# Windowed attention ahead of two expert layers: the transposes move into the scores' banks

## The chip, the cores and the metric

One core of one Trainium2 chip. The metric is the device time of one execution in microseconds (us), the median over the runs shown. Engines: PE is TensorE (PEld its weight loads), DVE is VectorE, ACT is ScalarE, POOL is GpSimd, SP is the engine that issues most DMAs.

## The reference, cut to what matters

```python
def _attn_ref(q, k, v):                       # (2, 8, 576, 64) each
    scores = (1 / np.sqrt(D)) * np.matmul(q, k.transpose(0, 1, 3, 2))
    # heads 0-3: 0 <= i - j < 32; heads 4-7: 0 <= i - j < 128 and (i - j) % 4 == 0
    scores = np.where(masks[None], scores, -1000000000.0)
    scores = scores - np.max(scores, axis=-1, keepdims=True)
    attn = np.exp(scores)
    attn = attn / (np.sum(attn, axis=-1, keepdims=True) + 1e-09)
    return np.matmul(attn, v)
def _moe_ref(x, domain_probs, w1, w2):        # x: 1152 x 512, 4 experts of 1024
    p = domain_probs / (domain_probs.sum(-1, keepdims=True) + 1e-09)
    return sum(p[:, e:e + 1] * (np.maximum(x @ w1[e], 0) @ w2[e]) for e in range(4))
def _moe2_ref(x, w_in, w_out, a, b):          # 512 -> 2048 -> 512
    h = x @ w_in
    P = a[0] + a[1] * h + a[2] * h**2 + a[3] * h**3
    Q = 1 + abs(b[0]) * abs(h) + abs(b[1]) * h**2
    return (P / (Q + 1e-06)) @ w_out
# output = _moe2_ref(_moe_ref(attention, 1152 x 512))
```

## The kernel before, in words

The 1152 tokens are cut into three chunks c of 384, the 8 heads into four pairs p. Attention works on twelve units (c, p), one chunk and two heads each (j = 0, 1). Since every query sees only a short band of keys, a unit is cut into 6 blocks of 64 queries by 96 keys (pairs 0 and 1) or 8 blocks of 48 queries by 80 keys (pairs 2 and 3, whose keys are gathered with step 4). Two blocks lie above each other on the 128 partitions, so a unit's scores are 128 x 2 x 288 or 128 x 2 x 320 values.

A unit goes through these steps, methods of `Attn`: `load` and `load_values` (SP issues the DMAs of queries with keys, L199, and of values, L206); `scores` on PE (L217) into the two PSUM banks `ps_s`, one a head; `masked` on DVE (L230), which adds a mask that is 0 or a large negative number and writes `pr` in SBUF; `maxima` on DVE (L240, and L241, which multiplies by minus the scale); `exps` on ACT (L248), one instruction a block pair and head, with the sums of the rows; `norm` (reciprocals on DVE, L255 and L256, two multiplications on POOL, L258); `transposes` of one head on PE (L269) into a bank of the pool `pso`; `copies` of that head back to SBUF, head 0 on DVE, head 1 on ACT (L275); `values` on PE (L286) into another `pso` bank; `split`, a rounded copy xh on ACT (L304, L311) and the rest xl = ps_v - xh on DVE (L306, L312).

PSUM has eight banks: two for `ps_s`, two for `pso` (tag "o", shared by transposes, value products and the output tiles `ps_o` of L363), four for the hidden layer `ps_h` (L326).

The order on every engine is that of the code, written by hand: an engine runs its instructions in the order in which the program issues them and waits in place. The units are pipelined over rounds r = 0 to 13 (L585): in round r unit r has its exponentials, unit r + 1 its scores, mask and maxima, unit r - 1 its transposes, unit r - 2 its value product and split. `keep_warm(n)` (L553) issues n dummy matmuls whose result nobody reads. Into the rounds are woven, by two tables, the first blocks of the next layer: `fill` (PE blocks of 12 matmuls, the hidden layer `h_k` and `hb`, L326, from round 3 on, and output tiles `o_tile`, L363, from round 8 on) and `prep` (splitting weights into a rounded part, L104, on DVE for the first two weight units and on ACT later, and a rest, L105, on DVE; and the loads of later weights). `late` is a list of deferred steps, among them the relu pair of L339 (hh, ACT) and L340 (hl, DVE); `run_late` issues what it holds.

After the last round the two expert layers run with the same blocks, PE nearly without a pause.

Of the kernel before, what the change touches and what calls it, by code (L numbers as in the profile page):

```python
# [18 lines left out]
F32 = mybir.dt.float32  # L19
# [15 lines left out]
TC = 384  # L35
# [9 lines left out]
def body(ctx, tc, qkv, mask, dp, w1, w2, w1d, w2d, coef, out):  # L45
# [45 lines left out]
    def split_w(store, nm):  # L91
        raws = {}

        def split(u, halves=(0, 1)):
            if u >= 2 * NG1:
                return
            if halves[0] == 0:
                raws[u] = store[u]
                store[u] = wp.tile([128, 2, 1024], F32R, tag=nm, name=nm)
            raw, w = raws[u], store[u]  # L100
            for i in halves:
                s = slice(i * 512, (i + 1) * 512)

                (nc.vector.tensor_copy if nm == "w1" and u < 2 else nc.scalar.copy)(w[:, 0, s], raw[:, s])  # L104
                nc.vector.tensor_tensor(  # L105
                    out=w[:, 1, s], in0=raw[:, s], in1=w[:, 0, s].bitcast(F32), op=ALU.subtract
                )
        return split
# [72 lines left out]
    class Attn:  # L181
# [5 lines left out]

        def __init__(self, c, p):
            self.c, self.p = c, p
            self.half = {}  # L190
            self.nb, self.qb, self.kb = BLOCKS[p // 2]
            self.n = self.nb // 2 * self.kb

# [31 lines left out]
            return t.rearrange("p (j i) -> p j i", j=2)  # L225

        def masked(self):
            pr = self.pr = ap.tile([128, 2, 320], F32, tag="pr", name="pr")[:, :, :self.n]
            m = mask_sb[:, 2 * (self.p // 2) + (self.c == 1), :self.n]
            nc.vector.tensor_tensor(  # L230
                out=pr, in0=ps_s[:, :, :self.n],
                in1=m.rearrange("p (o n) -> p o n", o=1).to_broadcast([128, 2, self.n]), op=ALU.add,
            )

        def blocks(self):
            return self.pr.rearrange("p j (i k) -> p j i k", k=self.kb)

        def maxima(self):
            mx, self.nmx = self.small("mx"), self.small("nmx")
            nc.vector.reduce_max(mx, self.blocks(), axis=AX.X)  # L240
            nc.vector.tensor_scalar_mul(self.nmx, mx, -QSCALE)  # L241

        def exps(self):
            self.total = self.small("total")
            pr = self.blocks()
            for j in range(2):
                for i in range(self.nb // 2):
                    nc.scalar.activation(  # L248
                        pr[:, j, i], pr[:, j, i], AF.Exp, scale=QSCALE, bias=self.nmx[:, j, i:i + 1],
                        accum_out=self.total[:, j, i:i + 1],  # L250
                    )

# [10 lines left out]

        def transposes(self, j):
            pr = self.blocks()
            ps = pso.tile([128, 512], F32, tag="o", name="ps_t")[:self.kb, :64 * self.nb]
            for i in range(self.nb // 2):
                n = 64 + self.qb
                nc.tensor.transpose(ps[:, i * 128:i * 128 + n], pr[:n, j, i], ident[:n, :n])  # L269
            self.half[j] = ps  # L270

        def copies(self, j):
            pt = ap.tile([96, TC], F32, tag=f"pt{j}", name="pt", bufs=2)[:self.kb]
            copy = nc.scalar.copy if j else nc.vector.tensor_copy
            copy(  # L275
                pt.rearrange("p (b q) -> p b q", q=self.qb),
                self.half[j].rearrange("p (b q) -> p b q", q=64)[:, :, :self.qb],
            )
            self.half[j] = pt

        def values(self):
            po = self.po = pso.tile([128, 512], F32, tag="o", name="ps_v")
            for b in range(self.nb):
                q = slice(b * self.qb, (b + 1) * self.qb)
                for j in range(2):
                    nc.tensor.matmul(  # L286
                        po[j * D:(j + 1) * D, q], lhsT=self.v[:, j, b], rhs=self.half[j][:, q],
                        start=True, stop=True,
                    )

        def split(self):
            po = self.po
            xh, xl = (t[:, self.p] for t in xt[self.c])
            if self.p < 2:
# [4 lines left out]
            else:  # L299
                src = po[:, :TC].rearrange("p (b i s q) -> p b (i s) q", b=2, i=2, s=2)  # L300
                dst = lambda t: t.rearrange("p (b q i) -> p b i q", b=2, i=4)
            if self.p >= 2 and self.c == 1:
                for b in range(2):
                    nc.scalar.copy(dst(xh)[:, b], src[:, b])  # L304
                for b in range(2):
                    nc.vector.tensor_tensor(  # L306
                        out=dst(xl)[:, b], in0=src[:, b], in1=dst(xh.bitcast(F32))[:, b],
                        op=ALU.subtract,
                    )
            else:  # L310
                nc.scalar.copy(dst(xh), src)  # L311
                nc.vector.tensor_tensor(  # L312
                    out=dst(xl), in0=src, in1=dst(xh.bitcast(F32)), op=ALU.subtract
                )


    hs = {}
# [158 lines left out]
    with tc.manual_schedule():  # L476
# [84 lines left out]
        units[2].load()  # L561
        load_w1(1, parts[:1])
        units[1].load_values()
        nc.scalar.dma_start(mask_sb[:, 1:], mask[:, 1:])
        nc.scalar.dma_start(dp_sb, dp)
        nc.scalar.dma_start(coef_sb, coef.to_broadcast([128, 6]))
        make_identity(nc, ident)
        nc.vector.memset(cbias, 1.000001)
        for c in range(NCH):
# [3 lines left out]
        def begin(r):  # L573
            if r < count:
                units[r].scores()
                units[r].masked()
                units[r].maxima()
            if 3 <= r + 3 < count:
                units[r + 3].load()

        keep_warm(8)
        begin(0)
        units[2].load_values()
        keep_warm(3)
        for r in range(count + 2):  # L585
            if r < count:
                units[r].exps()

            if r > 3 and r < count:
                units[r].norm()  # L590
            begin(r + 1)
            if r < 4:
                keep_warm((4, 8, 3, 3)[r])
            if r == 0:
                for u in range(2):
                    load_w1(u, parts[1:])
            if r > 1:
                units[r - 2].values()
                units[r - 2].split()
                if r + 1 < count:  # L600
                    units[r + 1].load_values()
            if r < 4:
                units[r].norm()
            run_late()
            late.extend(prep.get(r, ()))
            if r < 6:
                run_late()
            for f in fill.get(2 * r, ()):
                f()
            if 0 < r <= count:  # L610
                for j in range(2):
                    units[r - 1].transposes(j)
                    units[r - 1].copies(j)
            run_late()
            for f in fill.get(2 * r + 1, ()):
                f()
        run_late()
        x_pool.__exit__(None, None, None)
        attn_pool.__exit__(None, None, None)
# [195 lines left out]
def _mask():  # L815
# [4 lines left out]
    for kind, (nb, qb, kb) in enumerate(BLOCKS):  # L820
        a, k = np.arange(qb)[:, None], np.arange(kb)[None, :]
        band = (k > a) & (k <= a + WINDOW)
        for b in range(nb):
            i, o = divmod(b, 2)
            for edge in range(2):
                first = edge and (kind or b % 3 == 0)
                on = band & (k >= WINDOW) if first else band
                m[o, :qb, 2 * kind + edge, i * kb:(i + 1) * kb] = np.where(on, 0.0, -1e9 / QSCALE)
    return m.reshape(128, 4, 320).astype(bfloat16)


# [48 lines left out]
```

## Time and profile before

| | |
|---|---|
| time, median of 3 runs (lowest to highest) | 662.85 us (662.84 to 662.88) |
| the profiled execution's own time | 664.27 us |
| its span | 662.2 us |
| PE, PEld, DVE, ACT, POOL busy | 643.9, 575.5, 493.1, 273.7, 18.7 us |
| chain that ended last, by engine | PE 90%, DVE 5%, ACT 3%, issue 1% |
| DMA | 79.53 MB, mean 120 GB/s |

The profile is of one execution. Busy time is a sum over instructions; matmuls are pipelined and their ends are modelled, so a busy PE is not PE at its peak. "Granted clock" is the share of full TensorE speed that the chip granted. The chain of waits is followed back from the last instruction, at each step to what released it.

### The profile page before, as it was taken

The page shows a single profiled execution, that of the slowest core. Times are in us where ns is not written, and L with a number is a line of the kernel's source. Part 1 is how long each engine was busy: PE and PEld are TensorE (multiplying, and loading weights), DVE is VectorE, ACT ScalarE, POOL GpSimd, SP SyncE. Part 2 cuts the span into 40 slices and gives each one's busy share as a digit, 9 for nine tenths or more (in the row PEclk, how much of TensorE's full clock was granted, in tenths as well). Part 3 has the DMA queues.
Part 4 walks back from the last instruction along what each step waited for, and adds up shares of the span by engine and source line. Part 5 has one row for each costly group of instructions (what it writes and reads, how often), then busy time and mean ns, then how long its engine had stood idle before and what let it go on. Part 6 is the DMA issues. An engine that isn't in the chain of part 4 may idle for free.

```text
span 662.2 us, 9512 instructions
## 1 busy us (share of the span) xinstructions
PE 643.9 (97%) x3842; PEld 575.5 (87%) x3845; DVE 493.1 (74%) x716; ACT 273.7 (41%) x518; POOL 18.7 (3%) x30
## 2 busy tenths in 40 slices
PE   7788999999999999999999999999999999999997
PEld 3677879899999999999999999999999999999985
DVE  6766632886786786786786786535899999999986
ACT  4676511331431431431431422214665555555552
POOL 2311200000000000000000000000000000000000
PEclk8999999999999999999999999999999999999999
DMA  8953210454453454444444463530330330300012
GB/s 262 275 161 125 73 34 31 145 174 127 156 163 128 156 163 123 159 163 127 157 163 127 158 224 127 191 128 1 127 128 1 127 128 1 127 1 1 0 49 95
DMA packets 25419, 79.53 MB, mean 120 GB/s; under 512 B 2688, under 2 KB 2944, under 8 KB 23328
## 3 DMA queue, kind: packets, MB, share of 16 engines
q1 hardware_dynamic: 24800, 78.59, 36.4%
q8 instruction: 30, 0.49, 0.3%
q10 hardware_dynamic: 576, 0.35, 0.2%
q14 instruction: 13, 0.11, 0.0%
HBM read 59.79 MB, written 19.14 MB: 119 GB/s over the span
## 4 chain that ended last, share of the span: by engine, by line
PE 90%; DVE 5%; ACT 3%; issue 1%; ACTq 0%
PE ps_h L326 43%; PE ps_o L363 42%; ACT pr L248 3%; PE ps_t L269 1%; PE ps_h L553 1%; PE ps_v L286 1%; DVE mx L240 1%; DVE pr L230 1%; PE ps_h L408 1%; PE ps_s L217 1%; DVE xl L312 0%; PE ps_h L363 0%; ACT w L104 0%; DVE u L452 0%; DVE acc L393 0%
## 5 line engine op out<-in xcount | busy, mean ns | idle before, releaser
L326 PE MATMUL ps_h<-xh,w 128*128 128x384 f32 x1152 | 301.7, 336 | 0.3 <-DVE hl L340 0.3
L363 PE MATMUL ps_o<-w,hh 128*128 128x512 f32 x832 | 224.4, 391 | 0.0
L326 PEld LDWEIGHTS ps_h<-xh,w 128*128 128x128 f32 x1152 | 208.8, 188 | 2.2 <-DVE hl L340 0.5
L326 PE MATMUL ps_h<-xl,w 128*128 128x384 f32 x576 | 192.8, 335 | 0.0
L363 PEld LDWEIGHTS ps_o<-w,hh 128*128 128x128 f32 x832 | 155.1, 188 | 31.3 <-ACT hh L339 0.4
L363 PE MATMUL ps_o<-w,hl 128*128 128x512 f32 x416 | 128.7, 390 | 0.0
L326 PEld LDWEIGHTS ps_h<-xl,w 128*128 128x128 f32 x576 | 108.2, 188 | 1.2
L340 DVE SCALAR_TENSOR_TENSOR hl<-ps_h,hh 128x768 fp32r<-128x768 f32 x48 | 45.9, 957 | 68.9 <-ACT hh L339 68.9
L363 PEld LDWEIGHTS ps_o<-w,hl 128*128 128x128 f32 x416 | 78.0, 188 | 16.9 <-DVE hl L340 0.4
L339 ACT ACTIVATE hh<-ps_h 128x768 fp32r<-128x768 f32 x48 | 39.1, 815 | 119.9 <-PE ps_h L326 119.8
L167 ACT CAST w<-f 128x512 fp32r<-128x512 f32 x32 | 19.9, 621 | 123.6 <-DVE f L164 123.6
L387 DVE SCALAR_TENSOR_TENSOR acc<-ps_o,p_sb,acc 128x512 f32<-128x512 f32 x63 | 47.1, 748 | 11.4 <-PE ps_o L363 11.4
L105 DVE TENSOR_TENSOR w<-raw,w 128x512 fp32r<-128x512 f32 x64 | 42.9, 708 | 4.6 <-ACT w L104 4.5
L169 DVE TENSOR_TENSOR w<-f,w 128x512 fp32r<-128x512 f32 x32 | 22.2, 692 | 22.8 <-ACT w L167 22.8
L446 ACT ACTIVATE ab<-sq,cbias 128x768 f32<-128x768 f32 x24 | 22.7, 944 | 37.2 <-DVE sq L442 37.0
L104 ACT CAST w<-raw 128x512 fp32r<-128x512 f32 x60 | 34.0, 617 | 0.0
L437 ACT ACTIVATE sq<-ps_h 128x768 f32<-128x768 f32 x24 | 19.3, 803 | 32.4 <-PE ps_h L326 32.4
L248 ACT ACTIVATE pr<-pr,nmx 128x80 f32<-128x80 f32 (+1 forms) x84 | 29.6, 356 | 5.3 <-DVE nmx L241 5.3
L442 DVE SCALAR_TENSOR_TENSOR sq<-sq,absb,ab 128x768 f32<-128x768 f32 x24 | 24.3, 1011 | 3.8 <-ACT ab L438 3.8
L472 DVE TENSOR_TENSOR hl<-u,hh 128x768 fp32r<-128x768 f32 x24 | 22.9, 954 | 5.4 <-ACT hh L469 5.4
L452 DVE SCALAR_TENSOR_TENSOR u<-u,na,ps_h 128x768 f32<-128x768 f32 x24 | 24.4, 1015 | 0.8
L465 DVE SCALAR_TENSOR_TENSOR u<-u,na,sq 128x768 f32<-128x768 f32 x24 | 24.3, 1013 | 0.4
(64 smaller groups left out, 531.1 us busy)
## 6 DMA issues: line engine op xcount, KB each, us to landing
w<-w SPq DMA_DIRECT2D x32, 512.0 KB, 3.5
w<-w SPq DMA_DIRECT2D x16, 1024.0 KB, 4.9
raw<-in_w_dram SPq DMA_DIRECT2D x30, 512.0 KB, 5.7
x<-in_w1d_dram SPq DMA_DIRECT2D x16, 512.0 KB, 5.2
x<-in_w2d_dram SPq DMA_DIRECT2D x16, 512.0 KB, 5.0
out_dram<-acc SPq DMA_DIRECT2D x8, 256.0 KB, 2.2
v<-in_qkv_dram SPq DMA_DIRECT2D x6, 320.0 KB, 4.5
qk<-in_qkv_dram SPq DMA_DIRECT2D x4, 448.0 KB, 4.9
```

The costliest lines, as they stand in the source:

```text
L104: (nc.vector.tensor_copy if nm == "w1" and u < 2 else nc.scalar.copy)(w[:, 0, s], raw[:, s])
L105: nc.vector.tensor_tensor(out=w[:, 1, s], in0=raw[:, s], in1=w[:, 0, s].bitcast(F32), op=ALU.subtract)
L248: nc.scalar.activation(pr[:, j, i], pr[:, j, i], AF.Exp, scale=QSCALE, bias=self.nmx[:, j, i:i + 1], accum_out=self.total[:, j, i:i + 1],)
L326: nc.tensor.matmul(ps[:, i, :TC], lhsT=a[:, k, f], rhs=b[:, k], start=k + n == 0, stop=k + n == 5,)
L339: nc.scalar.activation(hh, ps[:, :, :TC], AF.Relu)
L340: nc.vector.scalar_tensor_tensor(out=hl, in0=ps[:, :, :TC], scalar=0.0, in1=hh.bitcast(F32), op0=ALU.max, op1=ALU.subtract,)
L363: nc.tensor.matmul(ps, lhsT=a[:, i, tk], rhs=b[:, i], start=v + n == 0, stop=v + n == 6)
L387: nc.vector.scalar_tensor_tensor(out=acc[t], in0=ps, scalar=pe, in1=acc[t], op0=ALU.mult, op1=ALU.add)
L442: nc.vector.scalar_tensor_tensor(out=self.sq, in0=self.sq, scalar=absb[:, 1:2], in1=self.ab, op0=ALU.mult, op1=ALU.add,)
L452: nc.vector.scalar_tensor_tensor(out=self.u1, in0=self.u1, scalar=na[:, 1:2], in1=ps, op0=ALU.add, op1=ALU.mult)
L465: nc.vector.scalar_tensor_tensor(out=self.u1, in0=self.u1, scalar=na[:, 0:1], in1=self.sq, op0=ALU.add, op1=ALU.mult)
L472: nc.vector.tensor_tensor(out=self.hl, in0=self.u1, in1=self.hh.bitcast(F32), op=ALU.subtract)
```

## The change

Both heads' transposes of a unit are issued in one piece into the two banks `ps_s` that hold scores, after the mask step of a later unit has read these, and one ACT copy takes both heads out into one tile `pt`. DVE takes no part in these copies any more. The mask step multiplies the scores by minus the scale as it adds a mask that is now 0 or 1e9; the maximum becomes a minimum of these negated values, the exponential runs with scale -1, and the scaling of the maxima (L241) is gone.

The rounds 0 to 3 get a loop of their own: there the exponentials of the two heads are issued apart, with the next unit's scores, mask and minima and the copy of a split between them, and the dummy matmuls are 8, 3, 0, 0 instead of 4, 8, 3, 3. In the later rounds `norm` stands ahead of the next unit's scores and mask, the minima behind the split, and the weight splits of `prep` behind the copy. In rounds 4 and 5 the transposes come ahead of the round's first fill block, later behind it.

At the start ACT's queue loads masks 0 and 2; masks 1 and 3, `dp` and `coef` are issued on SP in round 2, behind the queries of unit 6. Another hunk only gives a name to a condition in the weight split, and isn't shown.

```diff
@@ -187,7 +188,6 @@
 
         def __init__(self, c, p):
             self.c, self.p = c, p
-            self.half = {}
             self.nb, self.qb, self.kb = BLOCKS[p // 2]
             self.n = self.nb // 2 * self.kb
 
@@ -225,28 +225,29 @@
             return t.rearrange("p (j i) -> p j i", j=2)
 
         def masked(self):
+
             pr = self.pr = ap.tile([128, 2, 320], F32, tag="pr", name="pr")[:, :, :self.n]
             m = mask_sb[:, 2 * (self.p // 2) + (self.c == 1), :self.n]
-            nc.vector.tensor_tensor(
-                out=pr, in0=ps_s[:, :, :self.n],
-                in1=m.rearrange("p (o n) -> p o n", o=1).to_broadcast([128, 2, self.n]), op=ALU.add,
+            nc.vector.scalar_tensor_tensor(
+                out=pr, in0=ps_s[:, :, :self.n], scalar=-QSCALE,
+                in1=m.rearrange("p (o n) -> p o n", o=1).to_broadcast([128, 2, self.n]),
+                op0=ALU.mult, op1=ALU.add,
             )
 
         def blocks(self):
             return self.pr.rearrange("p j (i k) -> p j i k", k=self.kb)
 
         def maxima(self):
-            mx, self.nmx = self.small("mx"), self.small("nmx")
-            nc.vector.reduce_max(mx, self.blocks(), axis=AX.X)
-            nc.vector.tensor_scalar_mul(self.nmx, mx, -QSCALE)
-
-        def exps(self):
+            self.mx = self.small("mx")
+            nc.vector.tensor_reduce(out=self.mx, in_=self.blocks(), axis=AX.X, op=ALU.min)
             self.total = self.small("total")
+
+        def exps(self, js=(0, 1)):
             pr = self.blocks()
-            for j in range(2):
+            for j in js:
                 for i in range(self.nb // 2):
                     nc.scalar.activation(
-                        pr[:, j, i], pr[:, j, i], AF.Exp, scale=QSCALE, bias=self.nmx[:, j, i:i + 1],
+                        pr[:, j, i], pr[:, j, i], AF.Exp, scale=-1.0, bias=self.mx[:, j, i:i + 1],
                         accum_out=self.total[:, j, i:i + 1],
                     )
 
@@ -263,20 +264,17 @@
 
         def transposes(self, j):
             pr = self.blocks()
-            ps = pso.tile([128, 512], F32, tag="o", name="ps_t")[:self.kb, :64 * self.nb]
+            ps = ps_s[:self.kb, j, :64 * self.nb]
             for i in range(self.nb // 2):
                 n = 64 + self.qb
                 nc.tensor.transpose(ps[:, i * 128:i * 128 + n], pr[:n, j, i], ident[:n, :n])
-            self.half[j] = ps
-
-        def copies(self, j):
-            pt = ap.tile([96, TC], F32, tag=f"pt{j}", name="pt", bufs=2)[:self.kb]
-            copy = nc.scalar.copy if j else nc.vector.tensor_copy
-            copy(
-                pt.rearrange("p (b q) -> p b q", q=self.qb),
-                self.half[j].rearrange("p (b q) -> p b q", q=64)[:, :, :self.qb],
-            )
-            self.half[j] = pt
+
+        def copies(self):
+            self.pt = ap.tile([96, 2, TC], F32, tag="pt", name="pt", bufs=2)[:self.kb]
+            nc.scalar.copy(
+                self.pt.rearrange("p j (b q) -> p j b q", q=self.qb),
+                ps_s[:self.kb, :, :64 * self.nb].rearrange("p j (b q) -> p j b q", q=64)[:, :, :, :self.qb],
+            )
 
         def values(self):
             po = self.po = pso.tile([128, 512], F32, tag="o", name="ps_v")
@@ -284,11 +282,11 @@
                 q = slice(b * self.qb, (b + 1) * self.qb)
                 for j in range(2):
                     nc.tensor.matmul(
-                        po[j * D:(j + 1) * D, q], lhsT=self.v[:, j, b], rhs=self.half[j][:, q],
+                        po[j * D:(j + 1) * D, q], lhsT=self.v[:, j, b], rhs=self.pt[:, j, q],
                         start=True, stop=True,
                     )
 
-        def split(self):
+        def split(self, steps=(0, 1)):
             po = self.po
             xh, xl = (t[:, self.p] for t in xt[self.c])
             if self.p < 2:
@@ -299,19 +297,15 @@
             else:
                 src = po[:, :TC].rearrange("p (b i s q) -> p b (i s) q", b=2, i=2, s=2)
                 dst = lambda t: t.rearrange("p (b q i) -> p b i q", b=2, i=4)
+            parts = [(dst(xh), dst(xh.bitcast(F32)), dst(xl), src)]
             if self.p >= 2 and self.c == 1:
-                for b in range(2):
-                    nc.scalar.copy(dst(xh)[:, b], src[:, b])
-                for b in range(2):
-                    nc.vector.tensor_tensor(
-                        out=dst(xl)[:, b], in0=src[:, b], in1=dst(xh.bitcast(F32))[:, b],
-                        op=ALU.subtract,
-                    )
-            else:
-                nc.scalar.copy(dst(xh), src)
-                nc.vector.tensor_tensor(
-                    out=dst(xl), in0=src, in1=dst(xh.bitcast(F32)), op=ALU.subtract
-                )
+                parts = [tuple(t[:, b] for t in parts[0]) for b in range(2)]
+            for high, high32, low, src in parts:
+                if 0 in steps:
+                    nc.scalar.copy(high, src)
+            for high, high32, low, src in parts:
+                if 1 in steps:
+                    nc.vector.tensor_tensor(out=low, in0=src, in1=high32, op=ALU.subtract)
 
 
     hs = {}
@@ -561,9 +555,7 @@
         units[2].load()
         load_w1(1, parts[:1])
         units[1].load_values()
-        nc.scalar.dma_start(mask_sb[:, 1:], mask[:, 1:])
-        nc.scalar.dma_start(dp_sb, dp)
-        nc.scalar.dma_start(coef_sb, coef.to_broadcast([128, 6]))
+        nc.scalar.dma_start(mask_sb[:, 2], mask[:, 2])
         make_identity(nc, ident)
         nc.vector.memset(cbias, 1.000001)
         for c in range(NCH):
@@ -574,46 +566,70 @@
             if r < count:
                 units[r].scores()
                 units[r].masked()
-                units[r].maxima()
             if 3 <= r + 3 < count:
                 units[r + 3].load()
 
+        def turn(r):
+            if 0 <= r < count:
+                for j in range(2):
+                    units[r].transposes(j)
+                units[r].copies()
+
+        def run(n):
+            for f in fill.get(n, ()):
+                f()
+
         keep_warm(8)
         begin(0)
+        units[0].maxima()
         units[2].load_values()
         keep_warm(3)
-        for r in range(count + 2):
-            if r < count:
-                units[r].exps()
-
-            if r > 3 and r < count:
-                units[r].norm()
+
+        for r in range(4):
+            units[r].exps((0,))
             begin(r + 1)
-            if r < 4:
-                keep_warm((4, 8, 3, 3)[r])
+            if r == 2:
+                for i in (1, 3):
+                    nc.sync.dma_start(mask_sb[:, i], mask[:, i])
+                nc.sync.dma_start(dp_sb, dp)
+                nc.sync.dma_start(coef_sb, coef.to_broadcast([128, 6]))
+            units[r + 1].maxima()
+            keep_warm((8, 3, 0, 0)[r])
             if r == 0:
                 for u in range(2):
                     load_w1(u, parts[1:])
             if r > 1:
                 units[r - 2].values()
-                units[r - 2].split()
-                if r + 1 < count:
-                    units[r + 1].load_values()
-            if r < 4:
+                units[r - 2].split((0,))
+                units[r + 1].load_values()
+            units[r].exps((1,))
+            if r > 1:
+                units[r - 2].split((1,))
+            units[r].norm()
+            late.extend(prep[r])
+            turn(r - 1)
+            run_late()
+            run(2 * r)
+
+        for r in range(4, count + 2):
+            if r < count:
+                units[r].exps()
                 units[r].norm()
+            begin(r + 1)
+            units[r - 2].values()
+            units[r - 2].split()
+            if r + 1 < count:
+                units[r + 1].maxima()
+                units[r + 1].load_values()
             run_late()
+            if r < 6:
+                turn(r - 1)
+            run(2 * r)
+            if r > 5:
+                turn(r - 1)
             late.extend(prep.get(r, ()))
-            if r < 6:
-                run_late()
-            for f in fill.get(2 * r, ()):
-                f()
-            if 0 < r <= count:
-                for j in range(2):
-                    units[r - 1].transposes(j)
-                    units[r - 1].copies(j)
             run_late()
-            for f in fill.get(2 * r + 1, ()):
-                f()
+            run(2 * r + 1)
         run_late()
         x_pool.__exit__(None, None, None)
         attn_pool.__exit__(None, None, None)
@@ -825,7 +841,7 @@
             for edge in range(2):
                 first = edge and (kind or b % 3 == 0)
                 on = band & (k >= WINDOW) if first else band
-                m[o, :qb, 2 * kind + edge, i * kb:(i + 1) * kb] = np.where(on, 0.0, -1e9 / QSCALE)
+                m[o, :qb, 2 * kind + edge, i * kb:(i + 1) * kb] = np.where(on, 0.0, 1e9)
     return m.reshape(128, 4, 320).astype(bfloat16)
 
 
```

## Rows read from the trace of the kernel before

**Rows 1.** Windows: us, busy us by engine, PEclk, DMA share, GB/s.

```profile
0.00:98.88 98.88, 85.29 (x999) 67.17 (x1003) 61.67 (x125) 54.02 (x214) 18.67 (x30) 0.98 0.52 154
98.88:662.20 563.32, 558.66 (x2845) 508.32 (x2843) 431.46 (x591) 219.68 (x304) 0.00 (x0) 1.00 0.34 114
```

**Rows 2.** Chain of waits, first 100 us: start us, us, engine, tile, line.

```profile
7.27 2.27 ACT pr L248 x12
...
11.05 3.11 PE ps_h L553 x8
...
15.73 2.77 ACT pr L248 x16
...
20.10 0.66 PE ps_s L217 x24
...
21.75 0.92 PE ps_v L286 x24
22.67 2.31 PE ps_h L326 x12
...
26.21 2.27 ACT pr L248 x12
...
28.81 0.74 DVE pr L230
...
29.58 0.76 DVE mx L240
...
30.45 0.83 DVE xl L312
...
31.41 0.57 PE ps_t L269 x4
...
32.44 2.26 ACT pr L248 x12
...
38.74 2.88 ACT pr L248 x16
...
83.93 2.13 PE ps_h L326 x12
...
95.94 2.94 PE ps_o L363 x12
```

**Rows 3.** Timeline of PE: start us, us, [idle before it <- releaser].

```profile
60.70 0.36 PE L269 MATMUL ps_t<-ident,pr 112*80 112x112 f32 x2 [0.96 <-DVE xl L306]
...
91.49 0.36 PE L269 MATMUL ps_t<-ident,pr 112*80 112x112 f32 x2 [0.55 <-DVE acc L385]
```

**Rows 4.** Windows of the first rounds, columns as in rows 1.

```profile
8.00:10.00 2.00, 0.00 (x0) 0.00 (x0) 1.26 (x5) 2.00 (x13) 0.00 (x0) 1.00 0.97 376
...
12.00:14.00 2.00, 2.00 (x7) 0.68 (x5) 1.86 (x7) 0.00 (x0) 0.44 (x1) 0.50 1.06 254
...
16.00:24.00 8.00, 5.91 (x90) 4.41 (x91) 6.32 (x13) 6.46 (x34) 1.85 (x2) 1.00 1.03 339
```

**Rows 5.** Groups by line and shape, first 99 us: count, busy us, mean ns.

```profile
L340 DVE SCALAR_TENSOR_TENSOR hl<-ps_h,hh 128x768 fp32r<-128x768 f32 x6 | 5.7, 954 | 0.2 <-ACT hh L339 0.2
...
L339 ACT ACTIVATE hh<-ps_h 128x768 fp32r<-128x768 f32 x6 | 4.9, 815 | 0.5 <-PE ps_h L326 0.5
...
L275 DVE COPY pt<-ps_t 96x384 f32<-96x384 f32 x6 | 3.3, 548 | 0.1
...
L275 ACT COPY pt<-ps_t 96x384 f32<-96x384 f32 x6 | 2.8, 474 | 14.9 <-PE ps_t L269 14.9
```

**Rows 6.** Timeline, rounds 1 and 4: start us, us, engine, line, instruction.

```profile
11.25 0.81 DVE L230 TENSOR_TENSOR pr<-ps_s,mask_sb 128x640 f32<-128x640 f32 x1
...
29.01 1.15 ACT L104 CAST w<-raw 128x512 fp32r<-128x512 f32 x2
```

**Rows 7.** DMA issues, 10 to 24 us: KB each, median us to landing.

```profile
qk<-in_qkv_dram SPq DMA_DIRECT2D x2, 512.0 KB, 5.9
...
qk<-in_qkv_dram SPq DMA_DIRECT2D x1, 416.0 KB, 8.7
```

More of the change, by code (lines that the diff above doesn't have):

```diff
@@ L102, in split @@
                 s = slice(i * 512, (i + 1) * 512)
-                (nc.vector.tensor_copy if nm == "w1" and u < 2 else nc.scalar.copy)(w[:, 0, s], raw[:, s])
+                early = nm == "w1" and u < 2
+                (nc.vector.tensor_copy if early else nc.scalar.copy)(w[:, 0, s], raw[:, s])
                 nc.vector.tensor_tensor(
```

## The prediction

> **What bounds the kernel now.** I cut the span first at 98.88 us, where the first unbroken run of weight blocks starts [rows 1]. After it TensorE is busy 558.7 of 563.3 us; the change alters no instruction there, so that stretch can only start earlier. Before it TensorE is busy 85.3 of 98.9 us, part of it on dummy matmuls, so this stretch has slack. The chain of waits says what sets its pace [rows 2]. I write r for the round, exps(r) for the exponentials of unit r on ACT, T(r) for its transposes, C(r) for the copy that takes them out. From round 4 the chain is one loop: exps(4) starts at 26.21, DVE masks unit 5 at 28.81, reduces its maxima at 29.58, subtracts xl at 30.45, TensorE does the second half of T(3) at 31.41, and only after its copy does exps(5) start, at 32.44. The xl step is in it because T's two halves and the value product share two banks ("o"): the second half waits for xl to free one. exps(6) starts at 38.74, 6.30 later. From about 60 us the chain is nearly all TensorE, with such bank waits inside: 0.96 us at 60.70 and 0.55 at 91.49 [rows 3]. Last I looked at the clock in the first rounds: TensorE does nothing from 8 to 10 us, and the granted clock is 0.50 from 12 to 14 us, the 1.2 GHz level, where eight dummy matmuls take 3.11 us ahead of T(0) [rows 2, 4].
>
> **The change, part by part.**
>
> *Start of rounds 0 and 1.* The scaling instruction behind each maximum goes, so exps(0) starts at about 7.1 instead of 7.27 (in round 4 the step takes 0.11, from the maxima's end at 30.34 to xl at 30.45 [rows 2]). The mask step becomes a scalar_tensor_tensor: 0.954 us for 768 elements [rows 5] against 0.74 for 576 [rows 2], the same rate, so I price it as the old one. DVE masks unit 2 at 11.25, behind norm(0) and a weight half that follow exps(0) [rows 6]; so now at about 11.1 to 11.9. Now only three dummies stand before T(0), not eight, and T writes the scores' banks once masking has read them: T(0) runs 12.05 to 13.1. C(0) is new: one ACT copy of 768 elements from PSUM. The trace has 0.474 for 384 and 0.815 for 768 elements on ACT [rows 5], so it costs between 0.82 and twice 0.474; I take 0.82, of which 0.75 passes before the next ACT step. exps(2) starts at 13.95; it was 15.73.
>
> *Rounds 2 and 3.* On ACT: half of the exponentials (1.4), the xh copy, the other half (1.4), the copy (0.75). The xh copy waits for scores(r+1), which now waits for the earlier C, and for the values: 0.7 + 0.9 after that copy [rows 2] plus two hand-overs of 0.1, so it starts 1.8 into the round and ACT idles 0.4. Round 2: 1.8 + 0.4 + 1.4 + 0.75 = 4.35, exps(3) at 18.3.
>
> The Trainium skill, "Perfetto Trace Analysis", section Optimizing Tensor Performance, speaks against this part: independent groups should rotate through different PSUM banks so that taking one out overlaps the next matmuls. Here scores and transposes now meet in the same two banks. No run before shows that wait; what it would cost is rival 2.
>
> *Small loads.* Mask 1, which unit 4 needs, was loaded at the start on ACT's queue. Now it stands on SP behind the queries of unit 6, which wait for scores(3), done at 14.75: issue near 15.0. DMA is full in that stretch (share 1.03 from 16 to 24 us, 339 GB/s [rows 4]). Loads of 512 KB issued there land in 5.9 us, the slowest took 8.7 [rows 7]. About 181 KB of small loads no longer stand in front, 0.5 us at that rate: I take 15.0 + 5.9 - 0.5 = 20.4. DVE would mask unit 4 at 19.4 and now waits 1.0; T(2) then ends at 22.3 instead of 21.3, but ACT comes to C(2) only at 21.9, so 0.4 of the wait is paid. Bounds: 0 if it lands by 20.0, 3.7 if at 23.7. dp, coef and mask 3 follow it; DVE, POOL and ACT don't ask for those before round 5. What is queued behind them on SP are the values of unit 3, needed in round 5, so I cost that at nothing. exps(4): C(2) 22.4 to 23.1, so 23.1 against 26.21.
>
> *Rounds 4 and 5.* New loop: exps 2.27, to the mask 0.33, mask 0.77, hand-over 0.14, both halves of T 0.95 to 1.0 (one takes 0.57 with its start [rows 2]), 0.08, C 0.75, and then two weight casts. In the old order these lay in the wait for T: 1.15 us at 29.01 [rows 6]. Now they stand behind C on ACT and in front of exps(5): 1.1 on the path. Sum 6.4, where it was 6.23. So what leaves the loop (maxima 0.79, scaling 0.1, xl 0.83, the copy's 0.4) is given back by the other half of T, the larger copy and the casts. Round 5 the same with a wider mask and a small ACT step: 6.6 against 6.30. exps(5) 29.5, exps(6) 36.1 (was 38.74). DVE loses twelve copies of 0.548 [rows 5], off this path.
>
> *From round 6 on TensorE's own work decides.* T(4) ends at 29.5 + 2.27 + 0.33 + 0.8 + 0.14 + 1.0 = 34.05. Then a weight block of 2.2 (rows of 2.13 and 2.31 [rows 2]), scores 0.7, values 0.9, a block 2.2: 40.05. Unit 7's mask is done at 36.1 + 2.85 + 0.33 + 0.8 = 40.1, T(5) goes to 41.25. The next block needs the bank freed by DVE's hl, behind xl and the maxima: 40.1 + 0.55 + 0.8 + 0.95 = 42.4 (hl from [rows 5], xl as half its elements, the maxima from [rows 2]), a stall of 1.2. From 42.45 to the mark nothing should interrupt: eight blocks 17.6, six output tiles of 2.95 [rows 2] 17.7, six T 5.8, four scores 2.8, seven values of 0.9 to 1.1 6.95, together 50.85. The mark comes at 93.3 instead of 98.88: 5.6 us. The stalls of [rows 3] go with it, since T no longer takes an "o" bank; next late on TensorE is that hl.
>
> Sum: the profiled execution took 664.27 (span 662.2): 658.7. The median runs 1.4 below it, 662.85, so the prediction is **657.2**.
>
> **Rivals.**
>
> 1. *The loads set the pace.* For: DMA share about 1.0 from 8 to 24 us, and the mask's place behind it [rows 4, 7]. If it lands at 23.7, or the weights and queries of rounds 2 and 3 come no earlier than before, some 3 us of lead at exps(4) shrink to about 0.5 and only the later stalls are gained: 657.2 + 2.6 = 659.8; 660.9 with the whole 3.7. Against: scores(4) started at 20.10 behind TensorE's own work, with no load named, and fewer bytes stand in front.
>
> 2. *The shared banks decide.* In rounds 1 and 2 no block stands between T and the next scores, so TensorE idles about 0.9 and 1.7 us. If both waits fell wholly on the path, 657.2 + 2.6 = 659.8. Against: the exponentials of half a unit run meanwhile, and from round 3 on a block of 2.2 us covers a copy of 0.82.
>
> 3. *TensorE falls to 1.2 GHz (the other side: slower).* Rounds 2 and 3 lose their dummies and consist of small matmuls with idle of 0.9 and 1.7 us between. The trace shows such a fall after the idle 8 to 10 us. At that level blocks take 4.4 instead of 2.2. In round 3, T 0.25, block 2.2 and scores 0.3 less the 0.9 that TensorE had spare: about 1.85. Round 4: mask to mask 0.8 + 0.14 + 1.26 + 4.4 + 1.0 + 0.1 = 7.7 against 6.4, 1.3; round 5 0.6; round 6 has a block before T and one behind it, 4.8 and 2.2. Held to 45 us that is 10.7, so 657.2 + 10.7 = 667.9. It decides the sign if the low clock outlasts the block of round 6, near 40 us; if it ends in round 5 it costs 3.7, giving 660.9. Against: from 16 to 24 us the old kernel also idled, 5.91 busy of 8, with a clock of 1.00 [rows 4]. The Trainium skill, "TensorE: Matmul & The Clock Gate", section Why this matters for your kernels, says the same way round that idle stretches between bursts bring the lower clock back; the trace agrees with the fall to 0.50 behind the idle 8 to 10 us.
>
> **How the numbers follow.** Forecast 657.2: 0.63, its own range 654.2 to 659.3 (a TensorE without the hl stall and the mask's 0.4 gains 1.6 more; the rest is hand-overs of some 0.1 in a dozen rounds; a C of 0.95 costs 0.13 a round up to exps(6), 0.7). Rival 1: 0.20. Rival 2: 0.08. Rival 3: 0.09, half of it the short form. Range 654.2 to 661.2: it takes in rivals 1 and 2 and leaves out the long form of rival 3 and tails, some 0.15. What 0.2% is here, 1.3 us, is about what a measurement can tell from no change. Under 661.5: the forecast, nearly all of rivals 1 and 2 and half of 3, 0.88. Within: 0.06, the tails of 1 and of 3. Slower: 0.06, rival 3 held long.
>
> **What would show it.** Right: T of both heads in one piece with no xl before it; exps(2) near 14, exps(4) near 23, exps(6) near 36; casts between C and exps in rounds 4 and 5; C near 0.82; the first unbroken block run at 93. Rival 1: DVE or TensorE waiting for a DMA between 15 and 25 us, above all the mask step of unit 4. Rival 2: scores late behind C with ACT idle. Rival 3: a granted clock of 0.5 past 22 us, blocks of 4.4. The forecast is wrong if exps(4) stands at 25 or later, or if the stretch behind the mark is not 563.3 long.

## The result, and the profile after

The changed kernel takes 657.03 us (median of 4 runs, 656.59 to 657.91) against 662.87 (662.84 to 663.48) for the kernel before: ratio 0.9912, 95% interval 0.9894 to 0.9929. The forecast was 657.2, faster, range 654.2 to 661.2.

The two profiled executions are 664.27 and 656.59, so 7.68 us apart. Of 21 timed executions of the kernel before, six took 664.19 to 664.47 us at a mean granted clock of 0.996 to 0.997 and fifteen 662.42 to 663.69 at 0.998 to 1.000; the profiled one, with its fall of the clock in the first 16 us [rows 4], is like the six, and so 1.40 of the 7.68 is no gain of the change. Another 0.44 is that the profiled execution of after lies below its median. 7.68 - 1.40 - 0.44 = 5.84 is left between the medians.

Windows of the changed kernel, cut where the first unbroken run of weight blocks starts (columns as in [rows 1]):

```profile
0.00:91.05 91.05, 82.09 (x994) 67.49 (x996) 53.70 (x101) 57.87 (x214) 18.67 (x30) 0.98 0.53 168
91.05:654.60 563.55, 558.64 (x2845) 508.33 (x2843) 431.29 (x591) 219.86 (x304) 0.00 (x0) 1.00 0.34 114
```

Behind the mark nothing has changed (563.55 against 563.32 us [rows 1]). All of the gain is the mark at 91.05 instead of 98.88. The chain of waits of the changed kernel, up to the mark (start us, us, engine, tile, line):

```profile
7.30 2.27 ACT pr L249 x12
...
11.29 0.82 DVE pr L231
...
12.24 0.85 PE ps_s L270 x6
...
13.11 0.81 ACT pt L274
...
15.17 3.94 DMA mask_sb<-in_mask_dram
...
19.27 0.76 DVE pr L231
...
25.53 0.74 DVE pr L231
...
26.41 0.95 PE ps_s L270 x8
...
27.43 0.80 ACT pt L274
28.23 0.33 ACT w L105
...
29.27 2.17 ACT pr L249 x12
...
35.58 2.78 ACT pr L249 x16
...
40.68 0.87 DVE hl L334
...
41.60 2.36 PE ps_h L320 x12
...
47.76 0.77 PE ps_s L270 x8
...
91.05 16.66 PE ps_h L320 x96
```

What to see, beside [rows 2]: no xl stands ahead of the transposes; they are one piece of eight behind the mask step (26.41); the casts stand behind the copy (28.23); the loop from exps to exps is as long as before in round 4; and from 41.60 on nothing but TensorE is left. Then the clock, in windows of the changed kernel in rounds 2 and 3 (columns as in [rows 1]):

```profile
16.00:18.00 2.00, 0.70 (x6) 0.45 (x5) 1.48 (x5) 2.00 (x10) 0.00 (x0) 1.00 0.75 272
18.00:20.00 2.00, 1.77 (x44) 1.66 (x46) 1.97 (x3) 1.56 (x9) 1.85 (x2) 0.71 0.63 95
20.00:22.00 2.00, 2.00 (x18) 1.88 (x16) 1.32 (x3) 1.52 (x8) 0.00 (x0) 0.50 0.84 252
22.00:24.00 2.00, 2.00 (x13) 2.00 (x12) 1.56 (x4) 2.00 (x9) 1.05 (x2) 0.94 1.02 399
```

The granted clock was 0.71 from 18 to 20 us and 0.50, the 1.2 GHz level, from 20 to 22 us, after two microseconds in which TensorE was busy 0.70 of 2.00; in the next window it was back at 0.94. So the fall that rival 3 feared came, but it ended well before even the short form of that rival, which lasts to round 5. Groups of the changed kernel by line and shape in the first 91 us (count, busy us, mean ns):

```profile
L231 DVE SCALAR_TENSOR_TENSOR pr<-ps_s,mask_sb 128x640 f32<-128x640 f32 x6 | 4.8, 804 | 0.3 <-PE ps_s L217 0.3
L274 ACT COPY pt<-ps_s 80x768 f32<-80x768 f32 x6 | 4.8, 794 | 8.5 <-PE ps_s L270 8.5
```

The mask step costs what it cost (0.80 here, 0.81 at the same width in [rows 6]), and the copy of both heads 0.79, just under the lower bound of its price (0.82).

### The profile page after: what moved, and what is told of

Same layout as the page of the kernel before. It is cut to its first block, busy times and chain, and to the rows that moved or that the text cites. A ratio compares the mean times of both kernels' runs of the same rounds, so it can differ in the third digit from the quotient of the medians.

```text
span 654.6 us, 9485 instructions
## 1 busy us (share of the span) xinstructions
PE 640.7 (98%) x3837; PEld 575.8 (88%) x3838; DVE 485.0 (74%) x692; ACT 277.7 (42%) x518; POOL 18.7 (3%) x30
## 4 chain that ended last, share of the span: by engine, by line
PE 92%; DVE 4%; ACT 3%; DMA 1%; issue 0%; POOL 0%; SPq 0%; ACTq 0%; DVEq 0%; POOLq 0%
PE ps_h L320 45%; PE ps_o L357 43%; ACT pr L249 2%; PE ps_s L270 1%; PE ps_v L284 1%; PE ps_s L217 1%; DMA mask_sb<-in_mask_dram 1%; PE ps_h L402 1%; DVE pr L231 1%; PE ps_h L547 1%; PE ps_h L357 0%; ACT pt L274 0%; DVE mx L242 0%; DVE u L446 0%; DVE acc L387 0%
## 5 line engine op out<-in xcount | busy, mean ns | idle before, releaser
L170 DVE TENSOR_TENSOR w<-f,w 128x512 fp32r<-128x512 f32 x32 | 22.1, 692 | 23.1 <-ACT w L168 23.1
L249 ACT ACTIVATE pr<-pr,mx 128x80 f32<-128x80 f32 (+1 forms) x84 | 29.7, 357 | 5.3 <-DVE mx L242 5.3
```

Source lines behind the costliest of these rows:

```text
L249: nc.scalar.activation(pr[:, j, i], pr[:, j, i], AF.Exp, scale=-1.0, bias=self.mx[:, j, i:i + 1], accum_out=self.total[:, j, i:i + 1],)
```

## The experiments

Twelve runs; times are medians, ratios against runs of the kernel before on the same chip.

**Banks alone**

```diff
-            ps = pso.tile([128, 512], F32, tag="o", name="ps_t")[:self.kb, :64 * self.nb]
+            ps = ps_s[:self.kb, j, :64 * self.nb]
...
-            copy = nc.scalar.copy if j else nc.vector.tensor_copy     # one head
+            nc.scalar.copy(...)                                        # both heads
```

> The kernel before with one part alone: both heads' transposes into the scores' banks and one ACT copy; order, dummies, loads and scaling as before. Theory O (the gain is made by several parts, the order of the rounds above all): in round 1 nothing is won, since eight dummies still stand before T(0); exps(4) still near 26.2, since T(2) stands behind a weight block; rounds 4 and 5 lose xl, maxima and scaling from the loop but wait for the block, about 0.4 to 0.5 each; the bank stalls of 0.96 and 0.55 go. About 3 us in all: 659.9 (659.0 to 661.5). Rival B (the banks are the change, the rest is small): about 657, as the whole change. Rival S (the start makes the gain): within 1 us of 662.9.

658.25 us against 663.10 for the kernel before, ratio 0.9917 (0.9903 to 0.9930). Between the theories, nearer to B: banks and copy alone bring 4.85 of the whole change's 5.84 us. Chain of waits of the banks-alone kernel:

```profile
10.94 1.83 PE ps_h L550 x8
12.77 0.67 PE ps_s L269 x6
...
24.83 2.27 ACT pr L248 x12
...
36.36 2.88 ACT pr L248 x16
...
92.29 16.66 PE ps_h L323 x96
```

A window of the same kernel (columns as in [rows 1]):

```profile
12.00:14.00 2.00, 1.42 (x10) 0.84 (x8) 1.86 (x7) 0.54 (x1) 0.33 (x1) 1.00 1.04 276
```

Two things I had wrong. The same eight dummies take 1.83 here and 3.11 in [rows 2]: here the clock was 1.00 from 12 to 14 us, though TensorE was nearly idle from 8 to 10 us too (0.09 us busy). The fall in the profile of before is thus no fixed part of that start. And exps(4) starts at 24.83, not 26.2. But T(0) already starts 1.39 earlier than in [rows 2] (12.77 against 11.05 + 3.11 = 14.16), 1.28 of it by the shorter dummies. So this lead of 1.38 goes with the clock, and up to exps(4) the banks alone win nothing, as theory O had it. Their gain comes later: exps(6) starts 2.38 earlier (36.36 against 38.74), the mark 6.59 (92.29 against 98.88).

**Scaling in the mask step alone**

```diff
-            nc.vector.tensor_tensor(out=pr, in0=ps_s[...], in1=m, op=ALU.add)
+            nc.vector.scalar_tensor_tensor(out=pr, in0=ps_s[...], scalar=-QSCALE, in1=m, ...)
-            nc.vector.tensor_scalar_mul(self.nmx, mx, -QSCALE)
```

> The kernel before with one part alone: the mask step scales too and the scaling instruction behind the maxima is gone. Theory O: 0.1 to 0.2 us in each of the rounds 0 and 2 to 8 in which it lies on the chain, so 662.0 (661.5 to 662.6); the mask step costs 0.74 and 0.80 as before. Rivals B and S: no different, 662.5 or more.

661.60 us against 663.10, ratio 0.9976 (0.9966 to 0.9985): theory O, somewhat more than its 662.0. The trace bears on the clock too. The profiled execution took 662.84 and is one of three, of nine, with a mean clock of 0.996 to 0.997 (662.84 to 663.01 us); the other six, at 0.998 to 1.000, took 661.22 to 662.13. In the profiled one the fall is where [rows 4] have it:

```profile
12.00:14.00 2.00, 2.00 (x7) 0.68 (x6) 1.93 (x5) 0.00 (x0) 0.98 (x2) 0.50 1.09 284
```

This start is the same code as in the kernel before but for the scaling, so the fall goes with the longer of two times.

**Both of them, all else as before**

> The kernel before with two parts: transposes in the scores' banks with one ACT copy, and the scaling in the mask step; order of the rounds, dummies and small loads as before. Banks alone took 4.9 us off, the scaling alone 1.5. Theory P (the two parts carry the change, and the new order, dummies and loads together add nothing): they add up, 656.8 (656.2 to 657.6), the same as the whole change. Rival Q (the new order is needed for the last part): the scaling sits where ACT now waits for T, not for the maxima, so 658 or more.

658.34 us against 663.21, ratio 0.9925 (0.9908 to 0.9942). They don't add up: beside the banks the scaling is worth nothing that can be measured. Executions with a mean clock of 0.998 or more took 657.31 to 657.54 here (three) and 657.45 and 657.65 with the banks alone. In the chain of waits of this kernel T and its copy lead to the exponentials up to 30 us, and the maxima come in only at 33.52:

```profile
28.54 0.78 PE ps_s L269 x8
...
30.08 2.27 ACT pr L248 x12
...
33.52 0.82 DVE mx L241
```

Theory P falls. Rival Q's time came (658 or more); whether the new order adds anything to these two parts is not settled by it.

**All but the banks**

```diff
-            ps = ps_s[:self.kb, j, :64 * self.nb]
+            ps = pso.tile([128, 512], F32, tag="o", name="ps_t")[:self.kb, :64 * self.nb]
```

and a copy for each head, DVE and ACT.

> The changed kernel with the transposes back in the two banks that they share with value products and output tiles, and two copies, head 0 on DVE, head 1 on ACT; order, dummies, loads and scaling as changed. Theory O: the second half of T waits for xl again, but in rounds 4 and 5 xl now comes before the minima and the smaller copy saves 0.35, so exps(6) stands within 0.5 us of the changed kernel's 35.5; the stalls at the output tiles come back: 658.5 (657.5 to 660). Rival B: 661 or more. Rival S: 657 to 657.5.

663.75 us (660.88 to 666.18), ratio 1.0001 (0.9985 to 1.0017): in the median the whole gain is gone, as rival B had it. Timeline of PE in round 4 of the all-but-the-banks kernel (in brackets idle before it and its releaser):

```profile
28.72 0.58 PE L271 MATMUL ps_t<-ident,pr 112*80 112x112 f32 x4
30.68 0.55 PE L271 MATMUL ps_t<-ident,pr 112*80 112x112 f32 x4 [1.38 <-DVE xl L312]
31.00 0.42 PE L324 MATMUL ps_h<-xh,w 128*128 128x384 f32 x1
```

In the new order the weight block stands behind T, so the wait for xl holds up the block as well; in the old order the block ran ahead of it. I had only compared the loops on ACT. So in the median the new order and the rest win nothing without the new banks. A lower clock is part of this loss: it was 0.79 from 22 to 30 us in this trace, and ten of the twelve executions had a mean of 0.987 to 0.995. The two at 0.997 took 660.88 and 661.18, against 656.59 of the changed kernel at the same mean clock; what is left there, over 4 us, is the banks' share by this comparison.

**The start as before, whole and in halves**

```diff
-            keep_warm((8, 3, 0, 0)[r])
+            keep_warm((4, 8, 3, 3)[r])
...
-        nc.scalar.dma_start(mask_sb[:, 2], mask[:, 2])
+        nc.scalar.dma_start(mask_sb[:, 1:], mask[:, 1:])     # and dp, coef
```

The first of these three runs takes both pieces, the second the dummies alone, the third the loads alone; where the loads are early, those of round 2 are left out.

> The changed kernel with its start as before: masks 1 to 3, dp and coef loaded at the start on ACT's queue, dummies 4, 8, 3, 3. Theory O: scores(2) wait for their queries to 10.2, the clock falls, eight dummies take over 3 us, T(0) near 14, exps(2) near 16 instead of 13.8; two us that nothing returns: 659.0 (658.3 to 659.8). Rival S: 661 or more. Rival B: 657 to 657.5.

659.85 us, ratio 0.9944 (0.9931 to 0.9957). The size is as theory O had it (a little more), the reason isn't: T(0) starts at 12.94 in this chain, against 12.24, not near 14. The same kernel's chain of waits, from T(0) to round 3, is where the loss is looked for:

```profile
12.94 0.67 PE ps_s L270 x6
...
20.25 1.39 PE ps_h L547 x3
21.64 1.50 PE ps_v L284 x24
...
23.17 0.05 ACT xh L305
```

> The changed kernel with dummies 4, 8, 3, 3 as before; small loads stay late. Theory D (in the kernel with both put back it was the three dummies ahead of the values in rounds 2 and 3 that cost, 0.75 us and 1.39 us at the lower clock, since xh and the second half of the exponentials wait for the values): 659.2 (658.5 to 660). Rival L (the early small loads cost it): 657.0 to 657.6.

659.12 us (657.08 to 660.09), ratio 0.9926 (0.9910 to 0.9942). By itself this is no clean test of the dummies: in its profiled run scores(4) wait 1.86 us for a DMA and unit 4's mask step 1.49 for its mask, and the two executions with a mean clock of 0.998 took 657.08 and 657.75.

> The changed kernel with masks 1 to 3, dp and coef loaded at the start on ACT's queue; dummies 8, 3, 0, 0 stay. Theory D: scores(2) start near 10.2 instead of 9.0, but unit 2 is masked at 11.3 behind DVE's weight half either way, so 657.2 (656.5 to 657.8). Rival L: 659 or more.

657.27 us (657.14 to 657.60), ratio 0.9906 (0.9893 to 0.9919). Theory D: this run and the one with both put back differ in the dummies alone, and their intervals lie apart, so the dummies are the cost. How they cost is read from the chain above: three of them 1.39 at the lower clock, ahead of the values for which xh and half of the exponentials wait. The place of the small loads is not the cost, in the median. These four executions lie within 0.5 us.

**Casts ahead of the copy, and hl ahead of xl**

```diff
+            if r < 6:
+                late.extend(prep.pop(r))
             run_late()
```

> The changed kernel with the weight splits of rounds 4 and 5 ahead of T and its copy, as in the kernel before. If the casts lie on the path as the prediction priced them (1.1 us each behind the copy), exps(6) comes earlier: in round 5 ACT is free for 1.5 us before the copy and casts and absb fit, in round 4 only 0.5 is free behind xh. So exps(6) near 33.8 instead of 35.5 and 655.3 (654.5 to 656.2). Rival (something else sets rounds 4 and 5): 656.8 to 657.3.

658.56 us (656.30 to 659.93), ratio 0.9922 (0.9905 to 0.9939): not the forecast 655.3, but inconclusive on the casts. Its profiled run shows another loss first, unit 4's mask step waiting for its mask, and behind it the clock at 0.50 from 22 to 28 us. Timeline of DVE of the casts-first kernel:

```profile
22.32 0.76 DVE L231 SCALAR_TENSOR_TENSOR pr<-ps_s,mask_sb 128x576 f32<-128x576 f32 x1 [2.25 <-DMA mask_sb<-in_mask_dram]
```

```diff
             units[r - 2].values()
+            if r == 6:
+                run_late()
+                run(2 * r)
             units[r - 2].split()
...                      # further down both calls are left out in round 6
```

> The changed kernel with round 6's block ahead of the split and the minima, so that DVE does hl before xl and the minima. The profile of the changed kernel shows TensorE idle 1.13 us until that hl ends; the prediction counted 1.2. If this stall is on the path: 655.9 (655.3 to 656.6). Rival (the exponentials then come late instead, since xh waits behind the relu): 656.8 to 657.3.

658.84 us (657.38 to 659.64), ratio 0.9929 (0.9917 to 0.9942): inconclusive for the same reasons. Chain of waits of the hl-first kernel, the mask's DMA in it:

```profile
15.50 5.67 DMA mask_sb<-in_mask_dram
...
23.89 3.58 PE ps_h L320 x12
```

So rival 1's mask wait is there, in some executions and not in others: from issue to landing 3.94 us in the profiled run of the changed kernel, where DVE came to the mask step 0.16 behind it and had not idled, 5.67 and 6.31 in these two, where it waited.

**Dummies where TensorE idles**

```diff
-            keep_warm((8, 3, 0, 0)[r])
+            keep_warm((8, 8, 0, 0)[r])
...
                 units[r].copies()
+                keep_warm((3, 5)[r] if r < 2 else 0)
```

> The changed kernel with dummies where TensorE idles anyway: five more ahead of T(0), three behind T(0), five behind T(1); none ahead of the values. Theory K (the granted clock falls to 0.50 near 20 us in the changed kernel because TensorE idles in rounds 1 and 2, and this stretches values(1), T(2) and a block): the clock stays at 1.00 up to 30 us, exps(4) near 22.3 instead of 22.9, 656.2 (655.5 to 656.8), with less spread. Rival N (the fall is hidden behind the exponentials): 656.9 to 657.5, or more, since the dummies stand ahead of scores.

657.97 us (656.29 to 660.44), ratio 0.9925 (0.9908 to 0.9942). The clock does stay at 1.00 up to 30 us, but the time is no better: the mask landed at 20.91, exps(4) started at 23.61, and the clock fell later (0.83 from 30 to 40 us). Theory K's time falls; whether the fall of the clock costs anything is left open by this run.

**All of it, with an early mask, and the same without casts and hl**

```diff
-        nc.scalar.dma_start(mask_sb[:, 2], mask[:, 2])
+        nc.scalar.dma_start(mask_sb[:, 1:3], mask[:, 1:3])
```

with the dummies behind T, hl first in round 6, and round 5's casts ahead of its T.

> The changed kernel with dummies behind T, hl ahead of xl and the minima in round 6, round 5's weight splits ahead of its T, and mask 1 loaded at the start with mask 2 so that unit 4 never waits for it. By the prediction's terms (0.6 for the clock, 1.1 for hl, 1.1 for the casts of round 5, nothing for a mask that came in time): 654.3 (653.6 to 655.3). If TensorE is already full there: 656 or more.

655.74 us (655.35 to 656.89), ratio 0.9889 (0.9875 to 0.9903): above the forecast's 653.6 to 655.3, and the lowest median here, but the interval overlaps that of the changed kernel (0.9894 to 0.9929).

> The changed kernel with mask 1 loaded at the start and the dummies behind T, but round 6 and the weight splits as changed: the kernel of 655.7 without its two other parts. In the runs that tried hl first and casts first by themselves, unit 4's mask landed 2 to 3 us late and the clock fell, so their price is open. Theory H (those two are on the path once mask and clock are clean): 656.7 to 657.7, a us or more above that kernel, with a clock of 0.999. Rival (mask and clock alone made that kernel faster): 655.4 to 656.1.

656.84 us (656.58 to 657.37), ratio 0.9893 (0.9873 to 0.9913). The medians are 1.1 apart, as theory H had it, but the ratios only 0.0004, 0.3 us, and their intervals overlap; in this kernel's profiled run the clock fell near 33 us (a block of 3.65 in its chain), in the other's it stayed at 1.00. So the 2.2 of the two terms for casts and hl don't show, and what the two are worth, and their shares, is open. Here the one execution with a mean clock of 1.000 took 656.62, the five at 0.996 to 0.997 656.58 to 657.37: at most 0.75 us more at the lower mean clock.

## Why the prediction was right, and where it was not

*The loop.* Timeline of the changed kernel, the first instruction of exps(2) and of exps(4):

```profile
13.81 0.36 ACT L249 ACTIVATE pr<-pr,mx 128x80 f32<-128x80 f32 x1
...
22.93 0.38 ACT L249 ACTIVATE pr<-pr,mx 128x96 f32<-128x96 f32 x1
```

But for exps(0), which stayed where it was (7.30; forecast 7.1), it held step by step: exps(2) forecast 13.95, came at 13.81; exps(4) 23.1 and 22.93; exps(5) 29.5 and 29.17; exps(6) 36.1 and 35.48; the block behind hl 42.45 and 41.60. Rounds 4 and 5 took 6.24 and 6.31 (6.4 and 6.6 forecast; 6.23 and 6.30 before [rows 2]): what left the loop was given back, as forecast, by the copy, the casts and the other half of T.

*The banks.* More than half of the lead is made behind exps(6): it is 3.26 us there (35.48 against 38.74), the 1.40 that are no gain of the change among them, and 7.83 at the mark. The prediction had it so, 2.64 and 5.6. TensorE's waits show why. Waits of the kernel before, first 100 us (us in total, times, longest):

```profile
PE ps_t L269 <- DVE xl L312: 2.5, 3, 0.9
...
PE ps_t L269 <- DVE xl L306: 1.0, 1, 1.0
...
PE ps_t L269 <- DVE acc L385: 0.9, 2, 0.6
```

Windows from exps(6) to the mark, of the kernel before and of the changed one (columns as in [rows 1]):

```profile
38.74:98.88 60.14, 55.01 (x583) 46.06 (x572) 34.65 (x66) 32.06 (x120) 8.18 (x12) 1.00 0.29 86
```

```profile
35.48:91.05 55.57, 54.34 (x601) 46.72 (x600) 29.40 (x53) 33.96 (x120) 8.19 (x12) 1.00 0.31 99
```

TensorE idles 5.13 us there before and 1.23 after, 1.13 of it the wait for hl. In the changed kernel no transpose waits for xl or acc any more. With the banks alone none does either, and TensorE idles 1.72 us from exps(6) to its mark. With all but the banks both waits are back (1.5 and 1.2 us from 35 to 99 us).

*The start, mis-sized.* The step "exps(2) starts at 13.95; it was 15.73" counts 1.8 us, most of it for three dummies in place of eight. It rests on eight dummies in 3.11 us, which [rows 4] show at a clock of 0.50; without that fall eight take 1.83. So the profile of before stood 1.40 above the median for a reason that lies in the very step that the change shortens; the scaling-alone kernel, with the same fall and the same two levels of time, bears this out. The forecast took the gain from the profile and subtracted 1.4 as well: counted twice.

*TensorE's stretch, mis-sized the other way.* From 42.45 I counted 50.85 us; from 41.60 it took 49.45. Six T were priced at 0.97; in the chain they take 0.65 to 0.77, and the six together 4.39 instead of 5.8, which is the 1.4. The price was that of a T up to its end, for which a copy waits; the block behind it starts earlier (T at 26.41 takes 0.95, the next block starts at 27.12). With the earlier start, 0.85, the mark came 2.25 before the forecast 93.3.

*The balance.* 2.25 more gain up to the mark; against it 1.40 counted twice, 0.44 by which the profiled execution of after lies below its median, and 0.23 more behind the mark. 2.25 - 1.40 - 0.44 - 0.23 = 0.18, the distance from 657.2 to 657.03. That the time was met to 0.2 us is luck: errors of opposite sign nearly cancel, and each of the two large ones alone would have shown.

*The parts.* The prediction added its parts as if each had its own worth. They don't have one: banks alone bring 4.85, scaling alone 1.50, both 4.87, everything but the banks nothing in the median. Between banks with scaling (0.9925) and the whole change (0.9912) the intervals overlap, so what order, dummies and loads are worth together, some 1 us, isn't settled.

*Rival 1* had its mechanism right: the mask's wait shows in five of the profiled runs, between 0.21 and 2.25 us, and in the changed kernel's own profile the chain names the mask's DMA, but DVE lost nothing measurable to it; the rival's 2.6 us did not come. *Rival 2* is refuted: TensorE waits 0.89 and 1.52 us for the copies in rounds 1 and 2, and yet exps(4) is not late and the shared banks are what wins. Timeline of PE in the changed kernel, 13 to 22 us:

```profile
13.96 0.77 PE L217 MATMUL ps_s<-qk 64*48 64x80 f32 x32 [0.89 <-ACT pt L274]
...
18.23 0.73 PE L217 MATMUL ps_s<-qk 64*64 64x96 f32 x24 [1.52 <-ACT pt L274]
...
18.88 1.55 PE L284 MATMUL ps_v<-pt,v 96*64 96x64 f32 x24
...
20.36 1.72 PE L270 MATMUL ps_s<-ident,pr 112*80 112x112 f32 x8
```

The first two lines are the wait that the advice to rotate through banks would avoid (the Trainium skill, "Perfetto Trace Analysis", section Optimizing Tensor Performance). The measurement decides: banks that stand empty between mask step and next scores were better than two that values and output tiles also use. *Rival 3*: the fall came, but shorter than its short form, which lasts to round 5 and costs 3.7. The last two lines show it: values(1) took 1.55 instead of 0.92 and T(2) 1.72 instead of 0.95. It ended within the first whole block, which starts at 21.76, and exps(4) was not late by it (22.93, forecast 23.1). None of the four executions of the changed kernel had a mean clock above 0.997, so by that measure falls of at least this size are in all of them; what they cost is not shown.

## What to carry to other kernels

When a tile waits for a buffer that a later stage holds, look for one that is empty at that moment in an earlier stage: its price is a wait that a neighbouring block can cover. Parts of a change that shorten parallel ways into the same instruction don't add; price them in combination, and try each alone before crediting it. Before a sum is made against one profiled execution, ask whether that execution is typical, above all whether its clock fell where others' didn't.

## What the runs showed of the hardware that was not expected

Executions of one program differ in the granted clock: of 21 of the kernel before, six had a mean of 0.996 to 0.997 and fifteen of 0.998 to 1.000, and the six took about 1.5 us longer. Of the traces that share its start, the two in which the clock was 0.50 from 12 to 14 us (the kernel before, scaling alone) have TensorE idle 2.28 and 2.30 us ahead of scores(2), the two in which it stayed at 1.00 (banks alone, banks with scaling) 2.07 and 1.95. A load of 80 KB issued on SP between 14 and 16 us landed after 3.9 to 6.3 us in six traces. And with two loads on ACT's queue at the start, SP issued its third load of queries at 2.58 to 2.60 us in eight traces, with four loads there at 4.03 to 4.23 in six; why is not shown.
